# Softmax over k for batches 1 to 3, with agents on partitions instead of keys

## The chip, the cores and the metric

The kernel runs on one core of a Trainium2 chip. The metric is the device time of one execution in microseconds. A core has TensorE (matmuls; the profile calls it PE, and its weight loads PEld), VectorE (DVE), ScalarE (ACT), GpSimd (POOL) and SyncE (SP, which issues the DMAs). Matmul results go to PSUM, eight banks of 512 float32 columns on each of 128 partitions.

## The reference

Agent attention, and behind it a layer with h - tanh(h):

```python
scale = 1.0 / np.sqrt(q.shape[-1])
def sm(a, b):
    s = scale * (a @ b.transpose(0, 2, 1))
    s = s - s.max(-1, keepdims=True)
    e = np.exp(s)
    return e / (e.sum(-1, keepdims=True) + 1e-09)
agent_v = sm(agents, k) @ v          # 4 batches, 49 agents, 12480 keys, 128 channels
x = sm(q, agents) @ agent_v          # 4 x 12480 rows of q
h = x.reshape(-1, 128) @ w_in        # 128 x 2048
out = (h - np.tanh(h)) @ w_out       # 2048 x 128
```

## The kernel before

The foreground is the layer. The 49920 rows of q form 100 blocks of up to 500, 25 for each batch, and each block takes eight steps, 800 in all. A step (`m1`, `act`, `high`, `low`, `m2`) makes two tiles h of 128x500: four matmuls at L495 and L496, with the float32r high and low part of (agent_v @ w_in) as stationary side and the softmax of q (`pT`) streaming. ACT takes tanh (L505) and square (L507), DVE multiplies to g (L509), POOL rounds g to float32r (L538, gh), DVE subtracts (L543, gl), and six matmuls (L556 to L558) add the product with w_out into an accumulator. In one step of every second block four float32 matmuls (L554) do that instead. m2 runs about two steps behind m1. At a block's end ACT copies the accumulator out (L714).

PSUM is full: three buffers of two banks for h (`ph`), and two banks (`misc`) that the output accumulator, the scores of q (L451), the transposes for pT (L482) and all work below share.

The background is the softmax over k of the next batch, `phase1(b)`. For batch 0 it runs ahead of the loop, in a form of its own that the change leaves as it is. For batches 1 to 3 it is a list of jobs, run while the blocks of the batch before are computed. A job is a generator; each step advances every live job by one stage, right behind the step's m1 matmuls. Three jobs are started in each pair of blocks (16 steps), where `(pos + 2) % 16 in KS`. 98 tiles of 128 keys make 13 groups, twelve of eight tiles and one of two. The jobs of a batch are 13 of `scores`, then `max_in`, `max_out` and an empty place, 13 of `av`, `sums`, and four of `project`.

- `scores(g)`: the tile of k is the stationary side and the 49 agents stream (L269), so that keys lie on partitions and the eight tiles side by side, 392 columns. ACT copies them to s (L272), DVE takes the maximum over the tiles (L273).
- `max_in`, `max_out`: DVE reduces further, TensorE transposes (L284), DVE reduces over keys, and a matmul with ones (L295) spreads the 49 maxima over all partitions.
- `av(g)`, in four stages: POOL subtracts the maximum (L307), ACT takes exp (L309), TensorE multiplies with v (L325, into partitions 0 to 63 for even tiles and 64 to 112 for odd ones; a column of ones behind v gives the sums), DVE adds into acc (L356, L358).
- `sums`: DVE adds the two halves, divides by the sum, TensorE transposes (L390), and the result goes to `avs`.

The loads of k run two groups ahead and those of v three, on SP's queue; v has four buffers of its own. The order of instructions on each engine comes from a planner that works over a simulated timeline; what is written by hand is the order of jobs and stages and, for the first block, the order on three engines.

## Time and profile before

| | us |
|---|---|
| median of 3 runs | 2167.36 (2165.98 to 2169.63) |
| profiled execution, its own time | 2165.58 |
| its span, first to last instruction | 2163.8 |
| TensorE busy | 2136.6 (99%) |
| DVE busy | 2024.8 (94%) |
| ACT busy | 1801.7 (83%) |
| POOL busy | 1381.3 (64%) |

In the profile's rows, `out<-in` names what an instruction writes and reads by the program's tiles, then come the shapes and, behind x, the count. The ends of matmuls are modelled and they overlap in the pipe, so their spacing is read from their starts. A float32 matmul is two instructions, each with a weight load; a float32r matmul and a transpose are one.

### The profile page before, as it was taken

What the parts mean: (1) busy time and instruction counts of PE and PEld (TensorE: products, weight loads), DVE (VectorE), ACT (ScalarE), POOL (GpSimd) and SP (SyncE); (2) the same over time, 40 slices, a digit from 0 to 9 for tenths busy, and PEclk for the clock granted to TensorE, in tenths of its full rate; (3) what the DMA queues carried; (4) which work ended last, traced back from release to release, by engine and by line L of the source; (5) the groups of instructions that cost most, each with busy time, mean ns of one, the idle gap of its engine ahead of it and who ended that gap; (6) DMA issues with size and microseconds to landing.
All of it is one profiled execution on the core that took longest, in us unless ns stands there. A gap on an engine that the chain in (4) does not pass through costs nothing.

```text
span 2163.8 us, 30092 instructions
## 1 busy us (share of the span) xinstructions
PE 2136.6 (99%) x10712; PEld 1734.4 (80%) x10712; DVE 2024.8 (94%) x2037; ACT 1801.7 (83%) x2100; POOL 1381.3 (64%) x896
## 2 busy tenths in 40 slices
PE   8999999999999999999999999999999999999998
PEld 7588878777888887788788888777778888888886
DVE  7999999999999999899999999989999999999998
ACT  3887788888888788888888778888889888889897
POOL 0365567666655567676576556666666776767766
PEclk9999999999999999999999999999999999999999
DMA  9211102211111111112001110111010010000000
GB/s 347 87 59 58 61 29 65 61 51 39 39 39 58 51 59 48 58 44 65 29 20 59 58 51 20 49 60 50 20 38 21 20 39 20 29 29 20 29 10 21
DMA packets 65325, 108.68 MB, mean 50 GB/s; under 512 B 3984, under 2 KB 44176, under 8 KB 65168
## 3 DMA queue, kind: packets, MB, share of 16 engines
q1 hardware_dynamic: 65168, 106.68, 15.2%
q8 instruction: 88, 1.44, 0.3%
q14 instruction: 69, 0.57, 0.1%
HBM read 81.10 MB, written 25.56 MB: 49 GB/s over the span
## 4 chain that ended last, share of the span: by engine, by line
PE 86%; DVE 8%; POOL 3%; issue 2%; ACT 1%; DMA 0%; POOLq 0%; SPq 0%; DVEq 0%
PE h L495 15%; PE h L496 14%; PE misc L558 14%; PE misc L556 14%; PE misc L557 14%; PE misc L451 4%; DVE g L509 4%; PE misc L554 3%; POOL gh L538 3%; PE misc L269 3%; DVE gl L543 3%; PE misc L325 1%; PE h L243 1%; PE misc L482 1%; ACT y L505 0%
## 5 line engine op out<-in xcount | busy, mean ns | idle before, releaser
L538 POOL TENSOR_SCALAR gh<-g 128x1000 fp32r<-128x1000 f32 (+1 forms) x743 | 1192.7, 1606 | 633.9 <-DVE g L509 397.7
L543 DVE TENSOR_TENSOR gl<-g,gh 128x1000 fp32r<-128x1000 f32 (+1 forms) x743 | 977.7, 1317 | 85.7 <-PE misc L558 50.8
L505 ACT ACTIVATE y<-h 128x1000 f32<-128x1000 f32 (+1 forms) x800 | 798.9, 1002 | 204.6 <-PE h L496 199.7
L509 DVE TENSOR_TENSOR g<-h,z 128x1000 f32<-128x1000 f32 (+1 forms) x800 | 946.5, 1189 | 21.5 <-ACT z L507 19.6
L507 ACT ACTIVATE z<-y 128x1000 f32<-128x1000 f32 (+1 forms) x800 | 826.2, 1040 | 21.0 <-DVE g L509 3.9
L495 PE MATMUL h<-pT,awh 98*128 98x500 f32 (+1 forms) x1600 | 657.1, 411 | 0.0
L496 PE MATMUL h<-pT,awl 98*128 98x500 f32 (+1 forms) x1600 | 622.2, 389 | 0.0
L558 PE MATMUL misc<-gl,wo_h 128*128 128x500 f32 (+1 forms) x1486 | 588.4, 396 | 3.1 <-DVE gl L543 3.1
L556 PE MATMUL misc<-gh,wo_l 128*128 128x500 f32 (+1 forms) x1486 | 583.0, 392 | 4.5 <-POOL gh L538 4.2
L557 PE MATMUL misc<-gh,wo_h 128*128 128x500 f32 (+1 forms) x1486 | 577.8, 389 | 0.0
L495 PEld LDWEIGHTS h<-pT,awh 98*128 98x128 f32 x1600 | 300.9, 188 | 74.2 <-issue 14.6
L496 PEld LDWEIGHTS h<-pT,awl 98*128 98x128 f32 x1600 | 302.4, 189 | 69.4 <-issue 12.9
L556 PEld LDWEIGHTS misc<-gh,wo_l 128*128 128x128 f32 x1486 | 280.9, 189 | 69.5 <-POOL gh L538 16.5
L558 PEld LDWEIGHTS misc<-gl,wo_h 128*128 128x128 f32 x1486 | 279.5, 188 | 64.1 <-DVE gl L543 7.8
L557 PEld LDWEIGHTS misc<-gh,wo_h 128*128 128x128 f32 x1486 | 279.4, 188 | 55.2 <-issue 0.7
L462 POOL TENSOR_TENSOR qe<-qe,qm 126x392 f32<-126x392 f32 x50 | 70.7, 1414 | 64.1 <-ACT qe L460 64.1
L474 POOL TENSOR_TENSOR pp<-qe,pp 126x392 fp32r<-126x392 f32 x50 | 65.3, 1305 | 57.3 <-ACT pp L472 55.4
L451 PEld LDWEIGHTS misc<-ag,qt 128*126 128x126 f32 x800 | 96.3, 190 | 3.9
L451 PE MATMUL misc<-ag,qt 128*126 128x49 f32 x800 | 93.7, 269 | 0.0
L714 ACT ACTIVATE o<-misc 128x500 f32<-128x500 f32 (+1 forms) x100 | 58.1, 581 | 39.0 <-PE misc L554 24.6
L554 PE MATMUL misc<-g,wo_f 128*128 128x500 f32 (+1 forms) x196 | 90.2, 582 | 0.0
L269 PEld LDWEIGHTS misc<-ag,kt 128*128 128x128 f32 x588 | 71.9, 192 | 4.6 <-issue 1.8
(105 smaller groups left out, 875.4 us busy)
## 6 DMA issues: line engine op xcount, KB each, us to landing
kt<-kT SPq DMA_DIRECT2D x48, 512.0 KB, 3.6
qt<-qT SPq DMA_DIRECT2D x46, 500.0 KB, 3.4
outT<-o SPq DMA_DIRECT2D x46, 500.0 KB, 2.6
v<-v SPq DMA_DIRECT2D x36, 512.0 KB, 4.1
vt<-v SPq DMA_DIRECT2D x12, 512.0 KB, 7.1
raw<-w_in SPq DMA_DIRECT2D x4, 512.0 KB, 9.3
v<-w_out SPq DMA_DIRECT2D x4, 512.0 KB, 9.0
qt<-qT SPq DMA_DIRECT2D x4, 490.0 KB, 3.4
```

The lines of the kernel that those rows point to most:

```text
L451: nc.tensor.matmul(ps[:TT, t * A : (t + 1) * A], qt[:, at : at + TT], self.ag[:, b, :], start=True, stop=True)
L495: nc.tensor.matmul(h[:, c, :w], aw[0][:A2, sl], pT[:A2, :w], start=True, stop=False)
L496: nc.tensor.matmul(h[:, c, :w], aw[1][:A2, sl], pT[:A2, :w], start=False, stop=True)
L505: nc.scalar.activation(self.pair(y), h, AF.Tanh, scale=TSC)
L507: nc.scalar.activation(z, y, AF.Square)
L509: nc.vector.tensor_tensor(self.pair(g), h, self.pair(z), ALU.mult)
L538: self.nc.gpsimd.tensor_scalar(gh, g, 1.0, 0.0, ALU.mult, ALU.add)
L543: self.nc.vector.tensor_tensor(gl, g, gh.bitcast(F32), ALU.subtract)
L554: nc.tensor.matmul(acc[:, :w], wf[:, c * C : (c + 1) * C], gh[:, x], start=first, stop=last)
L556: nc.tensor.matmul(acc[:, :w], self.wo_l[:, f, :], gh[:, x], start=first, stop=False)
L557: nc.tensor.matmul(acc[:, :w], self.wo_h[:, f, :], gh[:, x], start=False, stop=False)
L558: nc.tensor.matmul(acc[:, :w], self.wo_h[:, f, :], gl[:, x], start=False, stop=last)
```

## The change

For batches 1 to 3 the scores are computed with the agents as stationary side, padded with zeros from 49 to 64 columns: four of the eight tiles of k stream into partitions 0 to 63 and four into 64 to 127, 512 columns side by side. The maximum is then one over columns: one number for each partition and group, and `max_in` merges the two halves on DVE; `max_out` falls away, its place in the job list stays. In `av` ACT takes exp in place with the negated, scaled maximum as bias, so POOL's subtraction falls away; four transposes bring keys back to partitions, ACT copies them to SBUF, and the matmuls with v follow in halves as before, now both of 64 columns. That is five stages instead of four. In `sums` a matmul with a 0/1 matrix `sel` adds the halves and transposes at once, a second spreads the sums, and DVE divides. Batch 0 keeps its form; its agents now lie 64 columns apart instead of 49.

```diff
-        self.ag = c.tile([128, B, A], F32, tag="ag", name="ag")
+        self.agz = c.tile([128, B, HALF], F32, tag="ag", name="ag")
+        self.ag = self.agz[:, :, :A]
         nc.sync.dma_start(self.ag, self.agT.rearrange("b c a -> c b a"))
+        nc.gpsimd.memset(self.agz[:, :, A:], 0.0)
...
-                st["s"] = self.keep.tile([128, NT * A], F32, tag="s", name="s", bufs=1)
-                st["mxp"] = self.small.tile([128, A, 2 * NG], F32, tag="mxp", name="mxp", bufs=1)
+                st["s"] = self.keep.tile([128, NG * 512], F32, tag="s", name="s", bufs=1)
+                if b == 0:
+                    st["mxp"] = self.work.tile([128, A, 2 * NG], F32, tag="mxp", name="mxp", bufs=1)
+                else:
+                    st["mxp"] = self.small.tile([128, NG], F32, tag="mxk", name="mxk")
...
-            for t in range(n):
-                nc.tensor.matmul(ps[:, t * A : (t + 1) * A], kt[:, t, :], self.ag[:, b, :], start=True, stop=True)
-            yield
-            pv = ps[:, : n * A]
-            nc.scalar.copy(st["s"][:, g * GT * A : (g * GT + n) * A], pv)
-            nc.vector.tensor_reduce(
-                st["mxp"][:, :, g], pv.rearrange("p (t a) -> p a t", a=A), axis=AX.X, op=ALU.max
-            )
+            w = n // 2 * 128
+            for c in range(n // 2):
+                for r in range(2):
+                    to = ps[HALF * r : HALF * (r + 1), c * 128 : (c + 1) * 128]
+                    nc.tensor.matmul(to, self.agz[:, b, :], kt[:, n // 2 * r + c, :], start=True, stop=True)
+            yield
+            nc.scalar.copy(st["s"][:, g * 512 : g * 512 + w], ps[:, :w])
+            nc.vector.tensor_reduce(st["mxp"][:, g : g + 1], ps[:, :w], axis=AX.X, op=ALU.max)
...
+            if b:
+                m = self.small.tile([128, 1], F32, tag="mk", name="mk")
+                top = self.small.tile([128, 1], F32, tag="mt", name="mt")
+                nc.vector.tensor_reduce(m, st["mxp"], axis=AX.X, op=ALU.max)
+                nc.vector.tensor_copy(top[:HALF], m[HALF:])
+                nc.vector.tensor_tensor(m[:HALF], m[:HALF], top[:HALF], ALU.max)
+                nc.vector.tensor_copy(m[HALF:], m[:HALF])
+                st["mb"] = self.small.tile([128, 1], F32, tag="mn", name="mn")
+                nc.vector.tensor_scalar(st["mb"], m, -SCALE, None, ALU.mult)
+                return
...
+            if b:
+                w = n // 2 * 128
+                e = st["s"][:, g * 512 : g * 512 + w]
+                nc.scalar.activation(e, e, AF.Exp, bias=st["mb"], scale=SCALE)
+                yield
+                ps = self.misc()
+                for c in range(n // 2):
+                    sl = slice(c * 128, (c + 1) * 128)
+                    nc.tensor.transpose(ps[:, sl], e[:, sl], self.ident)
+                yield
+                et = self.small.tile([128, 512], F32, tag="ke", name="ke")
+                nc.scalar.copy(et[:, :w], ps[:, :w])
+                yield
+                ps = self.misc()
+                for c in range(n // 2):
+                    for r in range(2):
+                        t = n // 2 * r + c
+                        k = rows(g, t)
+                        nc.tensor.matmul(
+                            ps[HALF * r : HALF * (r + 1), : C + 1],
+                            et[:k, c * 128 + HALF * r : c * 128 + HALF * (r + 1)],
+                            vt[:k, t, : C + 1],
+                            start=c == 0,
+                            stop=c == n // 2 - 1,
+                        )
+                yield
+                acc = st["acc"]
+                if g == 0:
+                    nc.vector.tensor_copy(acc, ps[:, : C + 1])
+                else:
+                    nc.vector.tensor_tensor(acc, acc, ps[:, : C + 1], ALU.add)
+                return
...
-            acc = an = st["acc"]
-            width = C + 1
-            half = self.small.tile([128, C + 1], F32, tag="half", name="half", bufs=1)
-            nc.vector.tensor_copy(half[:A, :width], acc[HALF : HALF + A, :width])
-            nc.vector.tensor_tensor(an[:A, :width], acc[:A, :width], half[:A, :width], ALU.add)
-            sm = self.small.tile([128, 1], F32, tag="sm", name="sm")
-            nc.vector.tensor_scalar(sm[:A], acc[:A, C : C + 1], EPS, None, ALU.add)
-            nc.vector.reciprocal(sm[:A], sm[:A])
-            nc.vector.tensor_scalar(an[:A, :C], an[:A, :C], sm[:A], None, ALU.mult)
+            acc = st["acc"]
             pt = self.misc()
-            nc.tensor.transpose(pt[:, :A], an[:A, :C], self.ident[:A, :A])
-            yield
-            nc.vector.tensor_copy(self.avs[:, b, :A], pt[:, :A])
-            nc.scalar.copy(self.avs[:, b, A:], pt[:, :A])
+            nc.tensor.matmul(pt[:, :A], acc[:, :C], self.sel, start=True, stop=True)
+            rows_of = acc[:, C : C + 1].broadcast_to([128, 128])
+            nc.tensor.matmul(pt[:, A:A2], rows_of, self.sel, start=True, stop=True)
+            yield
+            sm = self.small.tile([128, A], F32, tag="sm", name="sm")
+            nc.vector.tensor_scalar(sm, pt[:, A:A2], EPS, None, ALU.add)
+            nc.vector.reciprocal(sm, sm)
...
-        jobs = [scores(g) for g in range(NG)] + [max_in(), max_out(), None]
+        jobs = [scores(g) for g in range(NG)] + [max_in(), max_out() if b == 0 else None, None]
```

## Rows read from the trace of the kernel before

**Rows 1.** The page: busy time of each engine, and the chain by engine.
```profile
PE 2136.6 (99%) x10712; PEld 1734.4 (80%) x10712; DVE 2024.8 (94%) x2037; ACT 1801.7 (83%) x2100; POOL 1381.3 (64%) x896
...
PE 86%; DVE 8%; POOL 3%; issue 2%; ACT 1%; DMA 0%; POOLq 0%; SPq 0%; DVEq 0%
```

**Rows 2.** Stretches of two pairs each: with scores, with a@v, with neither.
```profile
core 0: us, PE busy (x) PEld busy (x) DVE busy (x) ACT busy (x) POOL busy (x), PEclk, DMA share, GB/s
144.30:233.10 88.80, 88.80 (x461) 74.75 (x460) 81.71 (x79) 71.87 (x85) 51.30 (x35) 1.00 0.19 59
360.00:446.40 86.40, 86.34 (x461) 68.75 (x460) 79.33 (x79) 72.84 (x85) 60.55 (x41) 1.00 0.19 56
1800.00:1878.30 78.30, 78.30 (x365) 64.03 (x364) 75.56 (x73) 69.84 (x79) 55.27 (x35) 1.00 0.08 27
```

**Rows 3.** Timeline of TensorE around one score group: start, duration, instruction.
```profile
1203.12 0.39 PE L496 MATMUL h<-pT,awl 98*128 98x500 f32 x1
1203.35 1.88 PE L269 MATMUL misc<-ag,kt 128*128 128x49 f32 x16
1205.05 0.47 PE L556 MATMUL misc<-gh,wo_l 128*128 128x500 f32 x1
1205.36 0.39 PE L557 MATMUL misc<-gh,wo_h 128*128 128x500 f32 x1
1205.59 0.39 PE L558 MATMUL misc<-gl,wo_h 128*128 128x500 f32 x1
```

**Rows 4.** Timeline of TensorE around one a@v group.
```profile
1368.55 0.39 PE L557 MATMUL misc<-gh,wo_h 128*128 128x500 f32 x1
1368.86 1.09 PE L325 MATMUL misc<-v,ke 128*64 128x129 f32 x16
1369.89 0.49 PE L495 MATMUL h<-pT,awh 98*128 98x500 f32 x1
1370.22 0.39 PE L496 MATMUL h<-pT,awl 98*128 98x500 f32 x1
```

**Rows 5.** Timeline of TensorE around four transposes for pT.
```profile
1210.83 0.40 PE L496 MATMUL h<-pT,awl 98*128 98x500 f32 x1
1211.07 0.42 PE L482 MATMUL misc<-identr,pp 126*98 126x126 f32 x4
1211.32 0.46 PE L558 MATMUL misc<-gl,wo_h 128*128 128x500 f32 x1
1211.62 0.39 PE L556 MATMUL misc<-gh,wo_l 128*128 128x500 f32 x1
```

**Rows 6.** Groups by line: count | busy us, mean ns | idle before.
```profile
L269 PEld LDWEIGHTS misc<-ag,kt 128*128 128x128 f32 x588 | 71.9, 192 | 4.6 <-issue 1.8
...
L482 PEld LDWEIGHTS misc<-identr,pp 126*98 126x98 f32 x400 | 39.6, 127 | 14.6 <-POOL pp L474 1.1 <-ACT o L714 0.4
...
L325 PEld LDWEIGHTS misc<-v,ke 128*49 128x49 f32 (+2 forms) x588 | 32.2, 130 | 15.4 <-issue 10.1 <-ACT z L507 2.5 <-DVE qe L469 1.1
...
L284 PE MATMUL misc<-ident,m 128*49 128x128 f32 x4 | 1.1, 274 | 1.4 <-DVE m L282 1.4
...
L390 PEld LDWEIGHTS misc<-ident,acc 49*128 49x128 f32 x3 | 0.4, 135 | 2.9 <-PE h L496 2.5 <-ACT y L505 0.4
```

**Rows 7.** Line L390: what TensorE's idle time before it waited for.
```profile
  DVE acc L388: 1.7, 2
```

**Rows 8.** Groups by line of POOL, DVE and ACT, with columns as in 6.
```profile
L487 ACT CAST pT<-misc 98x500 fp32r<-98x500 f32 (+1 forms) x100 | 56.8, 569 | 4.5 <-PE misc L482 3.3
L307 POOL TENSOR_TENSOR ke<-s,mb 128x392 f32<-128x392 f32 (+1 forms) x39 | 48.8, 1255 | 16.6 <-PE misc L325 16.0 <-DVE g L509 0.5
...
L273 DVE TENSOR_REDUCE mxp<-misc 128x49 f32<-128x392 f32 (+1 forms) x39 | 20.8, 534 | 0.2
L309 ACT ACTIVATE ke<-ke 128x392 f32<-128x392 f32 (+1 forms) x39 | 19.9, 511 | 5.9 <-POOL ke L307 4.5
L272 ACT COPY s<-misc 128x392 f32<-128x392 f32 (+1 forms) x39 | 18.0, 462 | 9.0 <-PE misc L269 9.0
...
L358 DVE TENSOR_TENSOR acc<-acc,misc 113x129 f32<-113x129 f32 x36 | 10.1, 281 | 1.7 <-PE misc L325 1.7
```

**Rows 9.** Waits in the a@v stretch of 2: waiter, releaser: us, times, longest.
```profile
POOL gh L538 <- DVE g L509: 15.6, 18, 3.7
...
DVE gl L543 <- POOL gh L538: 1.6, 2, 0.9
```

More of the change, by code (lines that the diff above doesn't have):

```diff
@@ L310, in av @@
             yield
-            if b == 0:
-                vt = ahead("v", load_v, g, 1)
-                if g == 0:
-                    ph = self.ph.tile([128, 2, 512], F32, tag="h", name="h")
-                    st["ps"], st["pr"] = ph[:, 0, :], ph[:, 1, :A]
-                ps, first, last = st["ps"], g == 0, g == NG - 1
-            else:
-                ps, first, last = self.misc(), True, True
+            vt = ahead("v", load_v, g, 1)
+            if g == 0:
+                ph = self.ph.tile([128, 2, 512], F32, tag="h", name="h")
+                st["ps"], st["pr"] = ph[:, 0, :], ph[:, 1, :A]
+            ps = st["ps"]
             flat = e3.rearrange("p t a -> p (t a)")
-            width = C if b == 0 else C + 1
             for t in range(n):
@@ L325, in av @@
                 nc.tensor.matmul(
-                    ps[HALF * odd : HALF * odd + w, :width],
+                    ps[HALF * odd : HALF * odd + w, :C],
                     flat[:r, t * A : t * A + w],
-                    vt[:r, t, :width],
-                    start=(first and t < 2),
-                    stop=(last and t >= n - 2),
+                    vt[:r, t, :C],
+                    start=(g == 0 and t < 2),
+                    stop=(g == NG - 1 and t >= n - 2),
                 )
             yield
-            if b == 0:
-                if g == NG - 1:
-                    em = st["em"]
-                    for i, (rhs, r) in enumerate(((em, 128), (e3[:, 0, :], 128), (e3[:, 1, :], TAIL))):
-                        nc.tensor.matmul(st["pr"], self.ones[:r, :], rhs[:r], start=(i == 0), stop=(i == 2))
-                    return
-                if g in (0, 1):
-                    return
-                if g in (2, 3):
-                    st["es", g % 2] = self.small.tile([128, GT * A], F32, tag="ke", name="es")
-                es = st["es", g % 2]
-                e0 = st["s"][:, (g - 2) * GT * A : (g - 1) * GT * A] if g in (2, 3) else es
-                nc.vector.tensor_tensor(es, e0, flat, ALU.add)
-                if g == NG - 2:
-                    es = st["es", 0]
-                    nc.vector.tensor_tensor(es, es, st["es", 1], ALU.add)
-                    st["em"] = self.small.tile([128, A], F32, tag="m", name="es")
-                    nc.vector.tensor_reduce(
-                        st["em"], es.rearrange("p (t a) -> p a t", a=A), axis=AX.X, op=ALU.add
-                    )
-                return
@@ L354, in av @@
-            acc = st["acc"][: HALF + A]
-            if g == 0:
-                nc.vector.tensor_copy(acc, ps[: HALF + A, : C + 1])
-            else:
-                nc.vector.tensor_tensor(acc, acc, ps[: HALF + A, : C + 1], ALU.add)
+            if g == NG - 1:
+                em = st["em"]
+                for i, (rhs, r) in enumerate(((em, 128), (e3[:, 0, :], 128), (e3[:, 1, :], TAIL))):
+                    nc.tensor.matmul(st["pr"], self.ones[:r, :], rhs[:r], start=(i == 0), stop=(i == 2))
+                return
@@ new lines, in av @@
+            if g in (0, 1):
+                return
+            if g in (2, 3):
+                st["es", g % 2] = self.small.tile([128, GT * A], F32, tag="ke", name="es")
+            es = st["es", g % 2]
+            e0 = st["s"][:, (g - 2) * GT * A : (g - 1) * GT * A] if g in (2, 3) else es
+            nc.vector.tensor_tensor(es, e0, flat, ALU.add)
+            if g == NG - 2:
+                es = st["es", 0]
+                nc.vector.tensor_tensor(es, es, st["es", 1], ALU.add)
+                st["em"] = self.small.tile([128, A], F32, tag="m", name="es")
+                nc.vector.tensor_reduce(
+                    st["em"], es.rearrange("p (t a) -> p a t", a=A), axis=AX.X, op=ALU.add
+                )
```

15 lines of the change are left out of this document (10 added, 5 removed).

## The prediction

> **What bounds the kernel now.** I read the page first. TensorE is busy 99% of the span and 86% of the chain that ended last lies on it; DVE has 8% of that chain, POOL 3%, ACT 1% [rows 1]. The second view is a table of stretches, to see what one background job costs where it runs. Each of the three stretches of [rows 2] begins and ends at the first m1 matmul of a pair of blocks and is two pairs long: one with six score groups, one with six a@v groups, one with neither. TensorE ran 461 instructions in the first two and 365 in the third, so 96 more, 16 for each group. The times are 88.8, 86.4 and 78.3 us: a score group lengthens the kernel by (88.8 - 78.3) / 6 = 1.75 us, an a@v group by (86.4 - 78.3) / 6 = 1.35 us. TensorE fills each stretch, at a granted clock of 1.00 (the 2.4 GHz level), while ACT has 72 and 73 of 89 and 86 us, POOL 51 and 61. DVE is nearest behind, with 82 of 89. So what TensorE's queue gains or loses in these jobs is gained or lost at the end, as long as the other engines keep their distance; the count of TensorE comes first, waits second.
>
> The third view is the timeline of TensorE around one group of each kind; a group's price is the time between two foreground matmuls before and behind it, less their own spacing of 0.227 (1205.36 to 1205.59 in [rows 3]).
> Scores now [rows 3]: from the last L496 at 1203.12 to L557 at 1205.36 is 2.24, less two spacings 1.78 us. That is the 1.75 of the stretches, so score groups bring almost no waits. Sixteen instructions (each float32 matmul is two) take about 0.11 each although only 49 columns stream: their weight loads, 128 columns wide, take 0.19 [rows 6], and that sets the pace.
> a@v now [rows 4]: from L557 at 1368.55 to L496 at 1370.22 is 1.67, less two spacings 1.21 us. It too has sixteen instructions, with 129 columns to stream, but its stationary sides are 64 or 49 columns and alternate between the two halves of the output partitions. 1.35 of the stretches less 1.21 leaves 0.14 us of waits for each a@v group.
>
> **The change part by part, on TensorE.** A batch has 13 groups, 12 of eight tiles and one of two; three batches are touched, so 36 full groups. For the three short ones I set the difference to nothing (four instructions each).
>
> Scores. The agents become the stationary side (64 columns, alternating halves) and the tile of k streams 128 columns: the instruction pattern of a@v, one column fewer. The nearest row is therefore the a@v group, 1.21 us, in which entering and leaving the half-array form is already contained. Saved: 1.78 - 1.21 = 0.57, times 36 = 20.5 us. Bounds: nothing saved (if the halves don't run together) and 20.5.
> Here a rule speaks against the row. The Trainium skill (TensorE: Matmul & The Clock Gate, Part 3, The mechanism) says that a weight load overlaps a running matmul only when its row group differs; all of these use all 128 rows. By that rule the halves would run one behind the other and the saving of 20.5 would not come. The trace disagrees: sixteen instructions of a@v whose loads take 0.13 each [rows 6] start and are followed by the next matmul within 1.03 us (1368.86 to 1369.89, [rows 4]). I go by the row.
>
> Transposes. Four more for each group, a float32 tile of 128x128 as stationary side. The nearest for the operation is the float32r transpose at L482: from L496 at 1210.83 to L556 at 1211.62 is 0.79, less two spacings 0.33 us for four [rows 5]. The float32 transposes L284 and L390 are one instruction each, four and three in all [rows 6], and the weight load of L390, 128 columns, takes 135 ns, like L482's 127 and unlike the 192 of the score matmul's 128 columns. So I take 0.33, times 36 = 12.0 us added. They start 0.06 apart (1211.07 to 1211.32). The upper bound is the pace of the score instructions, 0.11 each: 0.52 a group, 18.7 us; below 0.06 no row goes.
>
> a@v itself keeps count, width and halves: nothing, the same 1.21.
> Maximum and sums. One transpose and two short matmuls go and four short ones come for each batch: nothing, below 0.5 us. But TensorE waited for the normalised accumulator before its transpose at L390: 1.7 us in two waits [rows 7]. The new product with the selection matrix needs the last addition alone, so I count 1.7 us saved; bounds 0 and 1.7.
> Batch 0 now streams two strips of 49 columns instead of 98 in a row: its loads are those of 128 columns and set the pace, nothing.
>
> On the other engines, per group.
> POOL loses the subtraction, 1.26 us mean, 48.8 us in all [rows 8].
> DVE: the maximum over 512 instead of 392 columns is 0.53 [rows 8] times 512/392 at most, +0.16; the addition into acc is the same. The maximum's five small operations, at L358's 0.28 each, are 1.4 us three times in the run, in place of a like chain. With three score groups a pair that is 0.5 us more in a pair that gets 1.7 us shorter, where 3.5 us are free (88.8 - 81.7, halved): 1.3 stay free. The pairs without jobs have as little, (78.3 - 75.6) / 2 = 1.4 [rows 2], and TensorE never stands in them: nothing. If this cover goes, each score group costs what DVE is short of.
> ACT: the copy of the scores grows from 0.46 to 0.58 (500 columns at L487 are 0.57), the new copy behind the transposes is the same 0.58, and exp grows from 0.51 to at most 0.67 in proportion to its columns. What the bias operand costs no row shows: from nothing to a second exp's 0.51; I take nothing, since the operation goes through as many elements, and 0.7 for the whole exp as the upper middle [rows 8]. Together +0.12 for a score group and +0.8 for an a@v group (at most 1.2). A pair with three of the latter has 2.4 us more work on ACT where 6.8 of 43.2 us are free [rows 2]. So nothing for the sum, but the cover is worth naming: behind the two ACT operations queue the next tanh and square, behind these g, gh and gl, for which TensorE waits.
> PSUM: an a@v group takes a misc bank twice instead of once, the score group as before. One of the two banks belongs to the output accumulator nearly always. At one step (43.2 / 16 = 2.7 us) for each hold, an estimate, the other bank is taken for two steps by the scores of q, two by the transposes of blocks and six, not three, by a@v: 10 of 16 steps. The background jobs can wait; I count nothing.
> Transfers: none is added or moved past another. A v tile is held one stage longer, but its buffer is loaded again only when the second group behind it starts, some ten steps later: nothing. The larger score tile and the zeroed pad cost nothing after the start.
> Waits. The a@v groups have 0.14 us of waits each, 5.0 us in 36 groups. In that stretch POOL's gh is what comes late: the subtraction stood in its queue, and DVE's gl waited for gh 1.6 us there [rows 9]. With the subtraction gone I count 2 us saved; bounds 5 saved (all of it goes) and 4 lost (ACT's longer queue delays TensorE by 0.11 a group, about what POOL's did).
>
> The sum: -20.5 + 12.0 - 1.7 - 2 = -12.2 us. The profiled execution took 2165.6, so 2153.4; the median of the runs stands 1.8 higher, so I predict 2155 us.
>
> **The rivals.**
> Transposes at the pace of 128-column float32 loads: +6.7, so 2162. For it: no float32 transposes stand back to back in this trace. Against it: the 135 ns of L390's load.
> The gain comes back as waits in the a@v stretches, no change: 0.22 to 0.45 us of new wait for each of the 36 groups (8 to 16 us), 2163 to 2171. For it: the stage chain is one longer (exp, transposes, copy, product, sum), with two ACT operations in it between TensorE instructions that stand in order. Against it: ACT's copies in the score stretches cause next to no waits; TensorE fills those stretches. The same would come of DVE, if it runs short in the score stretches.
> Slower: the same place, one mechanism. TensorE reaches the transposes or the product before exp or the copy is done, because tanh and square of two steps stand ahead of them on ACT, and everything behind it on TensorE stands. It decides from 0.46 us a group (12.2 + 4.3 over 36); at one ACT operation of 0.6 for each group it gives +21.6 - 12.2, so 2177. For it: ACT's free share falls from 16% to about 10% in that stretch. Against it: the planner can move foreground matmuls between the stages.
> The change doesn't do what it says: halves that do not overlap in the score groups. Then sixteen at 0.11, the pace of today's score instructions [rows 3], and 0.2 for going in and out (0.08 before L325 and 0.10 behind the next matmul, [rows 4]) make 1.95 instead of 1.21: 26.6 us more, so 2182. [rows 4] speaks against it. It is what the rule of the Trainium skill named above gives.
> Better than forecast: all waits of the a@v stretches go and those of the steps beside them, 2145.
>
> **How the numbers follow.** What this kernel's measurement can tell from no change is about 0.2%, 4.3 us. Chances: forecast 0.52 (2149 to 2161), slow transposes 0.12, better 0.04, gain given back 0.15, slower by waits 0.14, no overlap 0.03. Faster by over 0.2% is the first three, 0.68; within 0.2% 0.15; slower 0.17. The range reaches from 2147 (all of the waits and a little more) to 2171 (the gain given back); outside it stay the slower cases and half of the better one.
>
> **What would show it.** Right: score groups that lengthen a pair by about 1.2 instead of 1.75 us, with two starts together each 0.11 us; four transposes 0.06 apart; a@v groups that lengthen it by about 1.55 to 1.65; pairs without jobs unchanged at 39.2 us; no wait before the product with the selection matrix. Wrong: transposes 0.11 apart; matmuls of the score groups 0.11 apart one by one; TensorE idle until exp or the copy in the a@v stretches, with ACT busy over 95% there; DVE filling the score stretches.

## The result and the profile after

The changed kernel takes 2174.36 us (median of 7 runs, 2171.79 to 2176.89), the kernel before 2168.17 beside it (7 runs): a ratio of 1.0029, 95% interval 1.0017 to 1.0041. It is slower by 0.29%; forecast were 2155 and a gain.

The page of the changed kernel (span 2172.6, against 2163.8), the lines that answer to [rows 1]:

```profile
PE 2137.4 (98%) x10859; PEld 1723.2 (79%) x10859; DVE 2016.0 (93%) x2031; ACT 1826.0 (84%) x2136; POOL 1345.4 (62%) x858
...
PE 92%; DVE 4%; ACT 2%; issue 1%; POOL 0%; DMA 0%; POOLq 0%; SPq 0%; DVEq 0%
```

TensorE's busy time rose by 0.8 us and the span by 8.8. The three kinds of stretches of [rows 2], two pairs of blocks each, after the change, in the table of stretches:

```profile
core 0: us, PE busy (x) PEld busy (x) DVE busy (x) ACT busy (x) POOL busy (x), PEclk, DMA share, GB/s
144.10:229.70 85.60, 85.60 (x462) 68.65 (x461) 81.75 (x79) 72.83 (x86) 54.51 (x36) 1.00 0.18 57
364.80:453.00 88.20, 88.20 (x487) 71.23 (x485) 79.73 (x79) 71.79 (x84) 53.29 (x35) 1.00 0.20 60
1808.90:1887.30 78.40, 78.40 (x366) 64.11 (x365) 75.67 (x73) 69.87 (x79) 55.06 (x35) 1.00 0.08 27
```

A score group now lengthens its pair by (85.6 - 78.4) / 6 = 1.20 us, where [rows 2] gave 1.75; an a@v group by (88.2 - 78.4) / 6 = 1.63 where it was 1.35; pairs without jobs are unchanged at 39.2. All three stand in the forecast's list of what would show it right, though the a@v pairs of this stretch hold no exp (it ran earlier, as shown below). So the loss lies elsewhere. I cut both traces at the first m1 matmul of each pair and summed the pairs by stage over the three batches:

| stage | forecast, us | measured, us |
|---|---|---|
| 13 pairs with scores | -20.5 | -20.8 |
| 4 pairs around the merged maximum (one with the first a@v groups) | 0 | +21.2 |
| 11 pairs with a@v (transposes +12.0, waits -2) | +10.0 | +8.0 |
| 10 pairs with sums and project | -1.7 | -1.9 |
| up to the first pair | 0 | +2.4 |
| the last 12 pairs | 0 | -0.1 |
| sum | -12.2 | +8.8 |

(The start varies by itself: -0.3 to +4.2 us against the kernel before in the executions below. A cut at m1 also lets m2 matmuls, 0.227 us each, pass from one stage into the next: here the score pairs hold 6 fewer of them than in the kernel before, those around the maximum 10 more and the a@v pairs 4 fewer.) The second line is what turned a gain into a loss. ACT's timeline in the first of these pairs (40.5 us in the kernel before, 47.6 now):

```profile
277.44 1.01 ACT L541 ACTIVATE y<-h 128x1000 f32<-128x1000 f32 x1 [0.18 <-PE h L532]
278.48 1.04 ACT L543 ACTIVATE z<-y 128x1000 f32<-128x1000 f32 x1
280.07 1.34 ACT L321 ACTIVATE s<-s,mn 128x512 f32<-128x512 f32 x2 [0.55 <-DVE mn L293]
281.32 0.99 ACT L541 ACTIVATE y<-h 128x1000 f32<-128x1000 f32 x1
282.21 6.51 ACT L321 ACTIVATE s<-s,mn 128x512 f32<-128x512 f32 x11
```

L321 is the new exp. All thirteen of a batch run here, right behind the merged maximum (`mn`), up to five pairs ahead of the transposes that use them: 6.51 us in which ACT does neither tanh (L541) nor square (L543). The table of stretches shows what this does to the other engines:

```profile
280.00:285.00 5.00, 5.00 (x24) 4.16 (x23) 4.07 (x5) 4.93 (x8) 3.70 (x2) 1.00 0.00 0
285.00:290.00 5.00, 2.38 (x11) 1.35 (x10) 0.49 (x1) 5.00 (x10) 0.00 (x0) 0.88 0.00 0
290.00:295.00 5.00, 3.49 (x17) 3.49 (x17) 3.77 (x4) 4.32 (x6) 2.21 (x2) 0.50 0.26 106
295.00:300.00 5.00, 5.00 (x15) 4.09 (x15) 3.08 (x4) 2.98 (x5) 3.27 (x3) 0.59 0.37 102
300.00:305.00 5.00, 5.00 (x24) 4.13 (x23) 4.96 (x8) 4.17 (x6) 1.03 (x1) 1.00 0.00 0
```

DVE does 0.49 us of work in the second stretch and POOL none; TensorE falls to 2.38 of 5, and behind that its granted clock is 0.50, the 1.2 GHz level, with 17 and 15 instructions in 5 us instead of 24. The table of waits for the pair (271.8 to 319.4) gives the chain, square, then g, then gh, and below it TensorE's own two waits:

```profile
POOL gh L574 <- DVE g L545: 14.2, 8, 8.2
DVE g L545 <- ACT z L543: 6.1, 3, 5.5
...
PE misc L518 <- ACT o L750: 2.5, 1, 2.5
...
PE misc L487 <- ACT pT L523: 1.6, 1, 1.6
```

TensorE's two waits end with the copy of the output (L750) and the cast of pT (L523). Both are ACT's, and both stood behind the row of exps.

The other rows that were forecast. TensorE around one score group, one a@v group and one set of transposes (as [rows 3 to 5], from three windows of its timeline):

```profile
210.25 0.39 PE L532 MATMUL h<-pT,awl 98*128 98x500 f32 x1
210.56 1.09 PE L277 MATMUL misc<-kt,ag 128*64 128x128 f32 x16
211.59 0.50 PE L594 MATMUL misc<-gl,wo_h 128*128 128x500 f32 x1
211.92 0.39 PE L592 MATMUL misc<-gh,wo_l 128*128 128x500 f32 x1
```
```profile
387.20 0.38 PE L532 MATMUL h<-pT,awl 98*128 98x500 f32 x1
387.52 1.11 PE L336 MATMUL misc<-v,ke 128*64 128x129 f32 x16
388.55 0.49 PE L594 MATMUL misc<-gl,wo_h 128*128 128x500 f32 x1
388.88 0.39 PE L592 MATMUL misc<-gh,wo_l 128*128 128x500 f32 x1
```
```profile
377.27 0.40 PE L593 MATMUL misc<-gh,wo_h 128*128 128x500 f32 x1
377.51 0.60 PE L326 MATMUL misc<-ident,s 128*128 128x128 f32 x4
377.86 0.47 PE L531 MATMUL h<-pT,awh 98*128 98x500 f32 x1
378.18 0.39 PE L532 MATMUL h<-pT,awl 98*128 98x500 f32 x1
```

By the forecast's reading (two foreground starts, less two spacings, 0.456): scores 211.92 - 210.25 - 0.456 = 1.21, as forecast; a@v 388.88 - 387.20 - 0.456 = 1.22, as forecast; transposes 378.18 - 377.27 - 0.456 = 0.45 instead of 0.33 (0.44 on average). In the trace's single records, which these rows merge, the transposes start 0.109 apart, not 0.063.

Groups by line, answering to [rows 6 to 8]:

```profile
L277 PEld LDWEIGHTS misc<-kt,ag 128*64 128x64 f32 x588 | 31.3, 136 | 15.7 <-issue 7.9 <-ACT z L543 5.3 <-ACT qe L500 1.1
L326 PEld LDWEIGHTS misc<-ident,s 128*128 128x128 f32 x147 | 18.4, 140 | 4.7
...
L416 PEld LDWEIGHTS misc<-sel,acc 128*128 128x128 f32 x6 | 1.1, 190 | 1.0 <-issue 0.9
```
```profile
L321 ACT ACTIVATE s<-s,mn 128x512 f32<-128x512 f32 (+1 forms) x39 | 23.6, 685 | 1.9 <-DVE mn L293 1.9
L279 ACT COPY s<-misc 128x512 f32<-128x512 f32 (+1 forms) x39 | 21.7, 556 | 1.9 <-PE misc L277 1.8
L329 ACT COPY ke<-misc 128x512 f32<-128x512 f32 (+1 forms) x39 | 21.6, 554 | 2.9 <-PE misc L326 2.9
```

The product with `sel` (L416) waits for no engine, exp takes 0.685 on average and the copies 0.55: as forecast.

### The profile page after: what moved, and what is told of

The parts are those of the page before. It is cut to its first block, busy times and chain, and to the rows that moved or that the text cites. A ratio compares the mean times of both kernels' runs of the same rounds, so it can differ in the third digit from the quotient of the medians.

```text
span 2172.6 us, 30335 instructions
## 1 busy us (share of the span) xinstructions
PE 2137.4 (98%) x10859; PEld 1723.2 (79%) x10859; DVE 2016.0 (93%) x2031; ACT 1826.0 (84%) x2136; POOL 1345.4 (62%) x858
## 4 chain that ended last, share of the span: by engine, by line
PE 92%; DVE 4%; ACT 2%; issue 1%; POOL 0%; DMA 0%; POOLq 0%; SPq 0%; DVEq 0%
PE h L531 17%; PE h L532 16%; PE misc L594 15%; PE misc L592 15%; PE misc L593 15%; PE misc L487 4%; PE misc L590 4%; PE misc L336 2%; PE misc L277 2%; DVE g L545 1%; PE h L248 1%; PE misc L518 1%; ACT s L321 1%; DVE gl L579 1%; PE misc L326 1%
## 5 line engine op out<-in xcount | busy, mean ns | idle before, releaser
L574 POOL TENSOR_SCALAR gh<-g 128x1000 fp32r<-128x1000 f32 (+1 forms) x743 | 1205.1, 1622 | 691.9 <-DVE g L545 397.0
L545 DVE TENSOR_TENSOR g<-h,z 128x1000 f32<-128x1000 f32 (+1 forms) x800 | 948.1, 1190 | 35.8 <-ACT z L543 30.5
L541 ACT ACTIVATE y<-h 128x1000 f32<-128x1000 f32 (+1 forms) x800 | 798.2, 1002 | 191.7 <-PE h L532 186.7
L543 ACT ACTIVATE z<-y 128x1000 f32<-128x1000 f32 (+1 forms) x800 | 827.6, 1041 | 17.9 <-DVE g L545 1.2
L487 PE MATMUL misc<-ag,qt 128*126 128x49 f32 x800 | 98.1, 277 | 4.7 <-ACT pT L523 4.7
L750 ACT ACTIVATE o<-misc 128x500 f32<-128x500 f32 (+1 forms) x100 | 58.0, 580 | 39.8 <-PE misc L590 29.3
L523 ACT CAST pT<-misc 98x500 fp32r<-98x500 f32 (+1 forms) x100 | 56.7, 568 | 5.3 <-PE misc L518 4.2
```

Of the source, the lines that this page charges most:

```text
L487: nc.tensor.matmul(ps[:TT, t * A : (t + 1) * A], qt[:, at : at + TT], self.ag[:, b, :], start=True, stop=True)
L541: nc.scalar.activation(self.pair(y), h, AF.Tanh, scale=TSC)
L543: nc.scalar.activation(z, y, AF.Square)
L545: nc.vector.tensor_tensor(self.pair(g), h, self.pair(z), ALU.mult)
L574: self.nc.gpsimd.tensor_scalar(gh, g, 1.0, 0.0, ALU.mult, ALU.add)
```

## The experiments

**Theory.** The row of exps costs the time: exp in place waits for no buffer and its bias is there for all groups at once, so the planner puts thirteen behind the maximum, and the layer's tanh and square behind them. **Rivals:** the transposes' slower pace, the new copy on ACT, or the two halves cost it.

**held_exp.** exp may not move ahead of its own stage:

```diff
+                mark, first = self.last_on(ET.Activation), self.count()
                 nc.scalar.activation(e, e, AF.Exp, bias=st["mb"], scale=SCALE)
+                self.hold(first, mark, (ET.Activation,))
```

> The changed kernel, with one ordering edge for each exp: behind the ACT instruction that was issued last before its own stage. Nothing is computed otherwise. Theory (the burst): the changed kernel loses 7.1, 5.1 and 8 us at the three places where 11 to 13 exps stand in one row on ACT, 20 us in all; spread over their stages that loss goes and the score groups' saving stays: 2174.4 - 20 = 2154, ratio to the kernel before 0.992 to 0.995. Rival (the loss lies in the a@v stretches: transposes, two holds of a PSUM bank, ACT's copies): moving exp changes less than 5 us, 2170 to 2175. Second rival (given back): exp, now inside the a@v stretches, delays tanh and square there by its 0.7 us: 36 x 0.3 to 0.5 us come back, 2165 to 2172.

Measured: 2168.14 us (11 runs), ratio 1.0006 (0.9997 to 1.0015): not the 2154 of the theory, but what the second rival named. The pair at 270 us is back at 40.5 us, so the row is gone with all it cost. But the eleven a@v pairs, 44.0 us each in the changed kernel, take 45.3, which gives back 15. Of these, 3.6 us are 16 more m2 matmuls that now fall into these pairs, and 8.7 are TensorE's idle time (waits of over 0.15 us; none in the changed kernel). The timelines of ACT, DVE and TensorE in one of these pairs:

```profile
427.94 1.04 ACT L545 ACTIVATE z<-y 128x1000 f32<-128x1000 f32 x1
...
432.06 0.59 ACT L331 COPY ke<-misc 128x512 f32<-128x512 f32 x1
432.53 1.06 ACT L545 ACTIVATE z<-y 128x1000 f32<-128x1000 f32 x1
```
```profile
428.86 1.38 DVE L507 TENSOR_TENSOR qe<-qe,qs 126x392 f32<-126x392 f32 x1
430.16 1.19 DVE L581 TENSOR_TENSOR gl<-g,gh 128x1000 fp32r<-128x1000 f32 x1
431.27 1.19 DVE L547 TENSOR_TENSOR g<-h,z 128x1000 f32<-128x1000 f32 x1
```
```profile
431.31 0.38 PE L534 MATMUL h<-pT,awl 98*128 98x500 f32 x1
432.61 0.47 PE L533 MATMUL h<-pT,awh 98*128 98x500 f32 x1 [0.92 <-DVE g L547]
```

Lines stand two lower in this kernel. TensorE stands from 431.31 to 432.61, 1.30 less its spacing of 0.23, for an h buffer that a g on DVE frees (431.27 to 432.46). The square of that g was done at 428.98; the g stood behind two other operations in DVE's queue, the normalisation of q's softmax (`qe`, 1.38 us) and a gl (1.19). Nine of the eleven pairs have one such stall, with the same order on DVE, 8.2 us together. ACT has a crowd at the same time: the cast of q's softmax (430.27), the copy of the output (430.70) and the new copy (432.06), with one tanh between them. I took this crowd for the cause, and the expectations of starts_moved and copy_on_dve below rest on that. The trace doesn't bear it out: the square that the crowd makes late starts at 432.53, when this g is over.

**one_buffer.** exp writes to a small buffer instead of in place, with no rule on its order:

```diff
-                e = st["s"][:, g * 512 : g * 512 + w]
+                e = self.small.tile([128, 512], F32, tag="kx", name="kx", bufs=1)[:, :w]
...
```

> The changed kernel, but exp writes a tile of its own with one buffer instead of writing in place, and no ordering edge. The next exp can then start only when the transposes of the group before have read it, so no row of exps can form. Theory (the burst comes of having no buffer to wait for): about the time of the held exps, 2152 to 2160, and the clock never falls behind the maximum. Rival (the edge itself reorders more than exp): one of the two stays above 2168. Second rival: one buffer makes exp wait for the transposes, and these for exp, 0.3 us a group: 2165.

Measured: 2169.05 us (11 runs), ratio 1.0007 (0.9998 to 1.0016): the time of held_exp, though not the 2152 to 2160 of the theory. Without any rule a wait for the buffer spreads the exps: nothing but their freedom to run early had made the row.

**before_in_place.** The same freedom given to the kernel before: its subtraction and exp in place.

```diff
-            e3 = sv if b == 0 else self.small.tile([128, GT, A], F32, tag="ke", name="ke")[:, :n]
+            e3 = sv
```

> The kernel before, with one edit: for batches 1 to 3 too the subtraction and exp write into s in place, instead of into a tile with two buffers. Theory (in-place work with no buffer to wait for is run as early as its operands allow): 13 subtractions of 1.26 us form a row on POOL behind the maximum, 16 us three times, and gh of the layer stands behind them; exps stand in twos and threes. TensorE loses 5 to 12 us each time: 2182 to 2200. Rival (the burst hurts only on ACT, where tanh and square are on the path; POOL has slack): within 4 us of 2168. Second rival (fewer waits for a ke buffer in the a@v stretches help): 2160 to 2165.

Measured: 2194.42 us (4 runs), ratio 1.0126 (1.0111 to 1.0142). POOL's timeline:

```profile
309.09 2.04 POOL L538 TENSOR_SCALAR gh<-g 128x1000 fp32r<-128x1000 f32 x2
311.09 13.25 POOL L307 TENSOR_TENSOR s<-s,mb 128x392 f32<-128x392 f32 x13
324.30 3.96 POOL L538 TENSOR_SCALAR gh<-g 128x1000 fp32r<-128x1000 f32 x3
```

The same row, on the engine that then had the first operation of the stage: 13.25 us without gh, and that pair takes 54.8 us instead of 43.2. The row belongs to in place, not to exp, its bias or the new layout.

**exps_spread, exps_slow.** The exps as a job of their own in `max_out`'s empty place, each held to its step: one in every step, or one in every third (two more `yield`).

```diff
-                nc.scalar.activation(e, e, AF.Exp, bias=st["mb"], scale=SCALE)
...
+        def exps():
+            for g in range(NG):
+                e = st["s"][:, g * 512 : g * 512 + tiles(g) // 2 * 128]
+                mark, first = self.last_on(ET.Activation), self.count()
+                nc.scalar.activation(e, e, AF.Exp, bias=st["mb"], scale=SCALE)
+                self.hold(first, mark, (ET.Activation,))
+                yield
...
```

> The changed kernel with its own job starts, but the exps are a job of their own in the place that max_out left: all 13 still run early, right behind the maximum, one in each step instead of in one row (an ordering edge for each). The a@v jobs keep their stages, without exp. Theory (the row of exps costs 20 us because tanh and square stand behind it; exp outside the a@v stretch costs that stretch nothing): the 21 us of the three places fall to about 3 us (13 steps, each 0.7 us of exp where 0.55 are free), a@v pairs stay at 44.1 us as in the changed kernel: 2174.4 - 18 = 2156. Rival (13 exps in 13 steps delay TensorE as much as in a row): 2170 or more. Second rival (the a@v pairs were fast in the changed kernel for another reason): pairs of 45.2, 2168.

> As exps_spread, but one exp every third step, so that the thirteen reach over some 2.4 pairs of blocks. Theory that ACT's free time over a pair is what failed: 39.15 us of a pair less ACT's own 34.9 leaves some 4.2 us, and 5.3 exps of 0.65 us in a pair take 3.4 of it, so they fit; no pair with exps is longer than 41 us, the stretches of a@v are as in after (44.05 a pair, they hold no exp), and the whole is 2154 to 2162. Rival, that exps at that early place cost as much however they are spread: 2170 or more.

Measured: 2174.23 us (6 runs; 1.0032, 1.002 to 1.0044) and 2170.38 us (11 runs; 1.001, 1.0001 to 1.0019). My expectation of exps_spread failed: without a row, with the granted clock at 0.997 on average instead of 0.992, the same is lost. The pairs from the maximum on take 135.9 us for three, 135.8 with the row and 131.6 in held_exp. A pair without jobs has 39.2 - 34.9 = 4.3 us free on ACT (half of the last of the three stretches above), and thirteen exps at one a step take over 8 us in less than a pair. Too much for ACT within a pair would account for the first two of the three pairs. It doesn't account for the third, the longest with 47.2 us: it holds no exp, ACT has 36.4 us of work in it, and TensorE's one wait there, 1.5 us, ends with DVE's g. exps_slow was to tell ACT's load from a cost of the early place as such, and its total came out on the rival's side of my numbers. Its pairs are divided (table of stretches of exps_slow; this execution took 2174.4, the longest of the 11):

```profile
274.30:316.00 41.70, 41.18 (x188) 32.38 (x186) 38.61 (x42) 35.58 (x43) 25.39 (x16) 1.00 0.10 36
316.00:362.90 46.90, 45.77 (x244) 35.39 (x245) 41.79 (x40) 40.04 (x49) 28.55 (x19) 1.00 0.15 45
...
407.50:453.80 46.30, 44.84 (x247) 35.36 (x243) 40.06 (x39) 35.80 (x42) 24.34 (x17) 1.00 0.19 57
```

The first, where exps run alone, is 41.7 us, close to held_exp's 40.5. In the second six exps run beside a@v and its copies, with ACT at 40.0 of 46.9, and TensorE has three short stalls, 1.1 us together; my forecast of 44.05 had left out that exps and copies would overlap. But the last pair shown holds no exp, has ACT at 35.8 of 46.3, and a stall of 1.4 us behind DVE's g. So ACT's load is not shown to be the whole of it.

**starts_moved.** held_exp, with the three starts of jobs in a pair moved from positions 2, 7 and 12 to 4, 11 and 15, so that the copy meets the cast and the output's copy elsewhere; **before_starts_moved** is the kernel before with the same.

```diff
-KS = (9, 14, 4)
+KS = (13, 1, 6)
```

> The kernel with held exps, and the three starts of background jobs in each pair of blocks moved from positions 2, 7 and 12 to 4, 11 and 15, so that exp and the copy of a group stand in steps in which ACT has no other background operation. In the held kernel one copy of three meets the cast of q and the copy of the output, and TensorE stands 1.1 to 1.3 us for an h buffer once in each a@v pair. Theory (the meeting of ACT operations makes that stall): it goes, 1.1 us x 12 pairs = 13 us, 2168 - 13 = 2155. Rival (ACT's total work in the stretch makes it, wherever it stands): within 4 us of 2168. Second rival (other meetings take its place, on PSUM banks or DVE): 2168 to 2180.

> The kernel before, with the job starts moved in the same way (4, 11, 15 instead of 2, 7, 12) and nothing else. If the positions help the changed kernel only, through its copy and exp: within 4 us of 2168. If they help any kernel (POOL's subtraction then stands apart from q's operations on POOL too): 2160 to 2164, and the gain of the moved starts has to be counted against this. It could also lose, where the subtraction now meets another operation: 2170 to 2175.

Measured: 2158.85 us (5 runs), ratio 0.9964 (0.995 to 0.9978), faster than both kernels and 9.3 us below held_exp; before_starts_moved 2167.92 (11 runs), ratio 1.0001 (0.9992 to 1.001). The starts alone are worth nothing in the kernel before. TensorE has no wait of over 0.15 us left in the a@v pairs. That doesn't show that ACT's crowd had made the stall: the order on DVE changed too, and in the four a@v pairs of the first batch a g now follows the normalisation directly, ahead of the gl. Where the 8 us of starts_moved lie, a table of stages below says.

**starts_moved_burst, exps_spread_moved, exps_slow_moved.** The moved starts with the row of exps left in (the changed kernel with the new KS and no more), with one exp a step, and with one in three steps.

> The changed kernel with nothing but the job starts moved to 4, 11 and 15; exps in a row as the planner puts them. Measures the row by itself against the starts_moved kernel (2158.9). Theory: 15 to 21 us more minus the 6 us that exps outside the a@v stretch save, 2170 to 2176; the moved starts do nothing for the row. Rival (the moved starts were what helped, not the edges): 2155 to 2162.

> The same, with the job starts at 4, 11 and 15 as well. If the stall of the held kernel came of exp and copy together, the moved starts have little left to gain here: 2153 to 2157. If the copy alone made it: another 5 to 10 us less than the spread exps. If the moved positions are worse for scores or the last a@v groups: up to 2162.

> exps_slow with the starts of starts_moved. If the meetings on ACT of the a@v stretch are copy with q's cast and output copy even without an exp there, moved starts save some us more: 2150 to 2158. If taking the exp out of the groups already removed the meetings: the same as exps_slow within 3 us.

Measured: 2182.51 (5 runs; 1.0066, 1.0052 to 1.008), 2170.21 (11 runs; 1.0012, 1.0003 to 1.0021), 2161.99 (7 runs; 0.9972, 0.9961 to 0.9983). The first two stand above every case expected of them, the third between its two. In one table, medians in us:

| place of exp | starts as before | starts moved |
|---|---|---|
| in a row behind the maximum | 2174.4 | 2182.5 |
| one a step behind the maximum | 2174.2 | 2170.2 |
| one in three steps | 2170.4 | 2162.0 |
| in its group's own stage | 2168.1 | 2158.9 |

(The kernel before took 2167.4 to 2168.5 beside them.) In the right column the time falls with each step by which the exps stand further apart; in the left one it doesn't from a row to one a step. That speaks against the early place as such, and for ACT's load within a pair only in part, by the pairs without exps above. With the moved starts the ordering edge by itself is worth 23.7 us (2182.51 to 2158.85). The profiled executions by the stages of the first table, each less the kernel before, in us; the column m2 has how many more m2 matmuls fall into the a@v pairs:

| kernel | scores | maximum | a@v | m2 | sums | span |
|---|---|---|---|---|---|---|
| as changed | -20.8 | +21.2 | +8.0 | -4 | -1.9 | +8.8 |
| held_exp | -20.7 | +2.0 | +23.2 | +12 | -3.4 | +0.8 |
| starts_moved | -18.6 | -3.5 | +18.4 | +30 | -3.7 | -7.5 |
| starts_moved_burst | -17.5 | +20.3 | +17.0 | +32 | -3.8 | +17.0 |
| starts_moved_buffer | -17.4 | -3.5 | +18.5 | +30 | -3.7 | -5.4 |
| starts_moved_rounded | -17.5 | -3.5 | +9.0 | +12 | -3.7 | -14.6 |

(The span has the start and the last pairs too.) The row costs 19 to 24 us in the pairs around the maximum, with either starts. Moving the starts brings held_exp 4.8 us in the a@v pairs although 18 more m2 matmuls (4.1 us) fall into them: with like work it is 8.9, about the idle time that went. It brings 5.5 around the maximum, where one a@v group (1.2 us) and 6 m2 matmuls (1.4) fewer stand, and costs 2.1 with the scores. With the row of exps left in, the a@v pairs take 9.0 more, but 36 more m2 matmuls (8.2 us) stand in them, so the table doesn't show in which stage the row got worse.

**copy_on_dve.** held_exp with the copy behind the transposes on DVE, since ACT seemed short:

```diff
-                nc.scalar.copy(et[:, :w], ps[:, :w])
+                nc.vector.tensor_copy(et[:, :w], ps[:, :w])
```

> The kernel with held exps, with the copy behind the transposes on DVE (an estimate of 0.65 us there, from the maximum's 0.648 over as many columns) instead of ACT's 0.58. DVE has 5 us free in such a pair. Theory (ACT's queue, met by the copy, makes the stall of 1.1 us a pair): the stall goes or is halved, 2155 to 2162. Rival (DVE is late as well, g and gl stand behind the copy): 2168 or more.

Measured: 2197.56 us (4 runs), ratio 1.014 (1.0124 to 1.0155). The a@v pairs take 46.7 to 48.5 us, and TensorE's idle time in them rises from 8.7 to 22.8 us, all but 0.4 of it behind DVE's g and gl. From 355 to 445 us DVE has 80.30 of 90.00 us and ACT 69.53. DVE was already the engine nearest behind TensorE and has less room than ACT. That is the rival's side, and it fits a stall that DVE's queue makes.

**transposes_twice.** held_exp with each transpose done a second time (extra work), for the price of a group's transposes:

```diff
+                for c in range(n // 2):
+                    sl = slice(c * 128, (c + 1) * 128)
+                    nc.tensor.transpose(ps[:, sl], e[:, sl], self.ident)
```

> The kernel with held exps, and each of the four transposes of a group done twice into the same place, so four more instructions of that kind in each of 36 groups. Prediction's price: 0.06 us each in a row, 0.25 for four, 36 x 0.25 = 9 us above the held exps. Rival (pace of 128-column float32 weight loads, 0.11 each): 0.44 for four, 16 us above. Second rival (transposes bring waits of their own): over 20 us above.

Measured: 2205.66 us (5 runs), ratio 1.0172 (1.0158 to 1.0186): 37.5 us above held_exp. Their own time is 0.44 x 36 = 16, and the other 21 come on top, as in the second rival. Of these, 7.1 are seen as idle time of TensorE in the a@v pairs (15.8 us instead of 8.7), and three of these pairs have a mean granted clock of 0.966; where the rest lies was not traced. In this stretch these transposes cost over twice their own time.

**transposes_rounded, starts_moved_rounded, starts_moved_buffer.** exp writes float32r, in a buffer of its own, and is transposed as float32r, on held_exp and on starts_moved (this rounds the weights that multiply v). The third has the buffer alone, in float32.

```diff
-                e = st["s"][:, g * 512 : g * 512 + w]
+                e = self.small.tile([128, 512], F32R, tag="kx", name="kx", bufs=1)[:, :w]
...
-                    nc.tensor.transpose(ps[:, sl], e[:, sl], self.ident)
+                    nc.tensor.transpose(ps[:, sl].bitcast(F32R), e[:, sl], self.identr)
```

> The kernel with held exps; exp writes a float32r tile of its own (rounded, so the weights of v lose low bits) and the transposes are float32r as those for pT. In the changed kernel float32 transposes start 0.109 us apart, in the transposes for pT 0.063. Theory (the type sets the pace): 0.06 apart, 4 x 0.045 x 36 = 6.5 us less, 2161. Rival (128 stationary columns set it, and the transposes for pT have 98): still 0.109 apart, 2168.

> starts_moved with exp written as float32r and transposed as float32r (the weights of v are rounded by it). By the pace seen in transposes_rounded (0.364 us a group against 0.438) 36 groups save 2.7 us: 2154 to 2157. If that pace was hidden by other waits of the a@v stretch: 2158 to 2160, as starts_moved.

> starts_moved with exp written to a buffer of its own (float32), transposes in float32: one of the two things that starts_moved_rounded changes. If its 8.4 us came from the buffer of exp (another order of the steps, one wait less): 2150 to 2155. If they came from the faster transposes, directly (2.7 us) and by waits that a shorter group no longer meets: 2157 to 2161, as starts_moved.

Measured: 2166.31 (11 runs; 0.9997, 0.9988 to 1.0006), 2150.49 (5 runs; 0.9917, 0.9903 to 0.993) and 2160.13 (5 runs; 0.9964, 0.995 to 0.9978). Four transposes in transposes_rounded:

```profile
431.69 0.39 PE L534 MATMUL h<-pT,awl 98*128 98x500 f32 x1
431.91 0.46 PE L328 MATMUL misc<-identr,kx 128*128 128x128 f32 x4
432.20 0.46 PE L533 MATMUL h<-pT,awh 98*128 98x500 f32 x1
432.50 0.39 PE L534 MATMUL h<-pT,awl 98*128 98x500 f32 x1
```

432.50 - 431.69 - 0.456 = 0.35 for a group, instead of 0.45; the single starts are 0.061 to 0.086 apart. On held_exp this saves 1.8 us (6.5 were expected; the measured pace gives 2.7). On starts_moved it saves 8.4 us, more than either of its expectations, and the buffer is not the reason (2160.13 against 2158.85). By the table of stages the a@v pairs fall by 9.5 us, from +18.5 to +9.0. About 2.5 of it is the transposes' own, and 4.1 are 18 m2 matmuls that now stand in the pairs with sums, which take no longer for them. Which waits made room for these, and the rest, was not traced.

**halves_in_turn.** starts_moved with the score matmuls in another order: first four tiles into the lower half, then four into the upper.

```diff
-            for c in range(n // 2):
-                for r in range(2):
+            for r in range(2):
+                for c in range(n // 2):
```

> The starts_moved kernel with the matmuls of a score group in another order: first the four tiles for partitions 0 to 63, then the four for 64 to 127, instead of alternating. Same work, same halves. Theory (alternating halves run two at a time, which is where the score groups save): the instructions of a half start 0.107 us apart one by one, a group takes 1.7 to 1.95 instead of 1.22, 36 x 0.5 to 0.7 = 18 to 26 us more: 2177 to 2185, slower than before. Rival (the 64-column weight load alone makes the saving): within 4 us of 2158.9.

Measured: 2177.05 us (5 runs), ratio 1.0046 (1.0032 to 1.0059), 18.2 us above starts_moved. One group:

```profile
207.11 0.39 PE L595 MATMUL misc<-gh,wo_h 128*128 128x500 f32 x1
207.44 1.58 PE L277 MATMUL misc<-kt,ag 128*64 128x128 f32 x16
208.95 0.50 PE L533 MATMUL h<-pT,awh 98*128 98x500 f32 x1
209.28 0.39 PE L534 MATMUL h<-pT,awl 98*128 98x500 f32 x1
```

209.28 - 207.11 - 0.456 = 1.71 instead of 1.21, and 36 x 0.50 = 18.0 is about what the kernel lost. In the single records the matmuls start one by one 0.109 apart at both ends of the group; the seven spacings around the change from one half to the other are 0.055 on average. So nearly the whole saving of the scores comes from the alternation of the halves: 1.71 is 0.07 below the old 1.78. The Trainium skill (TensorE: Matmul & The Clock Gate, Part 3, The mechanism) lets a weight load overlap a running matmul only where the row group differs; here all rows are used in both orders, and only the column half decides: the measurement contradicts the rule.

## Why the prediction was wrong

- **Scores, -20.5: right.** -20.8 in the trace, and halves_in_turn shows the mechanism; the rival in which halves do not overlap falls. (6 m2 matmuls, 1.4 us, have left these pairs; with like work it is -19.4.)
- **Transposes, +12.0: mis-sized.** 0.44 us a group instead of 0.33, so +15.8 us. I took the pace of a float32r transpose for a float32 one because the two weight loads last alike (135 and 127 ns); they do (140 ns), and the transposes are still 0.109 apart. Nor does the forecast's reading hold that the load's length sets the pace: the old score matmuls with loads of 192 ns start 0.112 apart, those of halves_in_turn with loads of 136 ns 0.109. The forecast's slow-transposes rival had this pace, at 0.52.
- **Sums, -1.7: right** (-1.9). **a@v waits, -2: right in sign.** 1.63 a group leaves nothing over 1.22 + 0.44, so the old 0.14 went. But those pairs hold no exp, so that +8.0 comes near the forecast's +10.0 is partly luck.
- **ACT, "so nothing for the sum": the step that failed.** I priced exp and copy in a pair with three a@v groups, 2.4 us where 6.8 were free. But exp did not run there: in place and with one bias for all groups, nothing tied it to its stage, and thirteen ran where the maximum came out, +21.2 us. held_exp, one_buffer and before_in_place show this from three sides, and so do the 23.7 us between starts_moved_burst and starts_moved. My slower rival had ACT as its place, and the order the other way round: tanh and square ahead of exp. It was exp ahead of tanh and square.
- **a@v waits, once exp is kept in its stage: wrong in held_exp.** Its a@v pairs take +23.2 us. The transposes of the 33 groups there are 14.5 and the 12 more m2 matmuls 2.7; the other 6.0 are waits, where the forecast had 2 fewer. It looked for such waits in ACT's queue, and the trace shows them behind DVE's g. With another time for the starts they are gone: +18.4 is 14.5, 30 more m2 matmuls (6.8) and 2.9 fewer waits, and the kernel stands 8.6 us below the kernel before in medians (2158.85 and 2167.43). The forecast's sum with the measured transposes, -20.5 + 15.8 - 1.7 - 2 = -8.4, comes to the same. The a@v terms agree with it; that the total does is partly luck, since the scores bring 1.9 us less and the pairs around the maximum are 3.5 us shorter.

What stays open: how the loss of a row divides between ACT's missing squares and the half clock behind it, why one exp a step loses as much as a row when some of the slow pairs hold no exp, which part of the moved starts removed the stall, and which waits the faster transposes removed.

## What to carry to other kernels

Price a changed stage where its instructions may run, not where the code has them: an operation in place whose inputs are ready for all groups at once has nothing to hold it back, and a scheduler may run them all together ahead of the work that feeds the bound engine. Free time of an engine summed over a stretch doesn't show that an added operation costs nothing: the order in its queue counts, and so does the order in the queues that feed the bound engine. When the bound engine stalls, follow the stall to the instruction that ended it and read that engine's queue; a crowd on another engine at the same time need not be the cause. After a change to a stage, try its starting positions again: they brought nothing before (1.0001) and 9 us once exp was held.

## What the hardware showed that I had not expected

- Float32 transposes of 128x128 start 0.109 us apart, float32r ones 0.061 to 0.086, with weight loads of the same length (140 ns).
- Matmuls into alternating column halves start in twos, about 6 ns and then 104 ns apart. With one half behind the other they start 0.109 us apart, but for the seven spacings around the change of halves (0.055 on average).
- TensorE's granted clock fell to 0.50 behind a stretch in which it was busy 2.38 of 5 us, and the foreground matmuls were then 0.415 us apart instead of 0.227. exps_spread, with a mean of 0.997 where the changed kernel has 0.992, lost as much time.
- exp of 128x512 with its bias read for each partition takes 0.709 us (median of its group in the changed kernel). The Trainium skill (ScalarE: Activation LUTs, What ACT_TABLE_LOAD costs) gives 280 ns and 0.833 ns an element for this form, an estimate of 707 ns by it: the trace agrees.
